# Group-major inputs, 112-row transfers and one decay load for two scans in a fused RWKV and MoE kernel

## The chip, the cores and the metric

The kernel runs on 1 core of one Trainium2 chip. The metric is the device time of one execution in microseconds (us), lower is better; the figure quoted is the median of several executions. TensorE (PE, with its weight loads shown apart as PEld), VectorE (DVE), ScalarE (ACT), GpSimd (POOL) and SyncE (SP, which here only issues DMA transfers) run side by side, each through its own list of instructions in order, and wait for one another by semaphores.

## The reference

A recurrence over 768 steps for 4 batches x 8 heads with a 40x40 state, and behind it two feed-forward blocks on 3072 tokens.

```python
for t in range(S):
    y[:, :, t] = np.einsum('bhd,bhde->bhe', rt, state)
    Sa = np.einsum('bhde,bhe->bhd', state, at)
    state_decay = state * wt[:, :, None, :] - np.einsum('bhd,bhe->bhde', Sa, bt)
    state = state_decay + np.einsum('bhd,bhe->bhde', vt, kt)
...
h = x @ w_in                                   # 3072x320 by 320x2048
x = (h * (1.0 / (1.0 + np.exp(-1.702 * h)))) @ w_out
...
h = (x @ w1) * (x @ w2) @ w3                   # 320x1024 twice, 1024x1024
out = h @ w_out2                               # 1024x320
```

## The kernel before

**The recurrence.** Time is cut into 12 chunks of 64 steps; a chunk of one batch is a group, so there are 48 groups (`NG`), numbered so that four groups in a row are the four batches of one chunk. A group's tiles hold two halves of 40 rows each, in partitions 0 to 39 and 64 to 103 (104 rows, with 24 unused ones between), and 4 head pairs x 64 steps = 256 columns per operand.

**L_part(n)** prepares the decays of group n. One transfer brings four operands of 256 columns: the decays shifted one way, the decays shifted the other way, a and b (`LA`, 104 rows of 4096 bytes, of which the DRAM array has all 48 groups side by side in each row). On DVE a scan (L453) multiplies the decays from the back, a product of 4 columns (L456) forms each head's whole decay, a reciprocal of 4 columns (L457) starts the second scan (L458), which multiplies reciprocally from the front. Then a is multiplied on POOL (L460) and b on POOL or DVE (L462, L464), the result goes to DRAM scratch (`psc`), and PE multiplies a by b into a triangular block (L476), which DVE or ACT copies out (L482, L479).

**T_part(blk)** inverts the triangular blocks of 8 groups on DVE: a transpose (L498), 30 pairs of products and sums (L514, L518), a transpose (L524), and then PE and ACT steps (L543 to L559). **J_part, V_part, S_pair** read the scratch back (`pq`, `xl`), load `jk`, `jr`, `kb`, `xy`, and run the recurrence itself, two groups at a time, on PE, DVE, ACT and POOL; S_pair's state and output are added on DVE (L732, L734) and the output is stored to DRAM (`ysc`).

**moe1(k)** is the first feed-forward block for chunk k: its input is loaded from `ysc` and split on ACT and DVE into a high and a low part (L903, L905, L915, L916); then for 16 slices f there are 8 matmuls (L958), a gelu on ACT (L962), a cast on ACT (L964), a remainder on POOL (L965), and 6 matmuls for the second layer (L942). Its result is transposed on DVE (L974). Its weights arrive as 64-bit numbers and are converted by DVE (L795, L797, L799), ACT (L793, L801, L808) and POOL (L810). **moe2(blk)** is the second block, six times 512 tokens; its matmuls (L1140, L1126) stand at the end of PE's list, behind all of the recurrence and moe1.

**What sets the order.** No engine's order is written by hand. `Plan.run` takes all operations with a cost, an engine, what each reads and writes, and a due time (`at`, made of constants such as `D1`, `TG`, `G1`, `JO`), and plays them through its own cost rules; the order in which it starts them is the order in which they stand on each engine. A transfer's cost comes from `us()`, which before is its bytes at one rate for all. So a changed cost or due time moves instructions everywhere.

All transfers but four stand on SP's one list, in the planner's order, and SP waits there for what a transfer needs.

Of the kernel before, what the change touches and what calls it, by code (L numbers as in the profile page):

```python
# [18 lines left out]
C = 64  # L19
# [28 lines left out]
G1 = 0.54  # L48
# [9 lines left out]
B1 = 0.45  # L58
# [47 lines left out]
def PO(n):  # L106
    return 0.18 + 2.15e-3 * n
# [6 lines left out]
class Plan:  # L114
# [173 lines left out]
def rwkv_moe_kernel(ctx: ExitStack, tc: tile.TileContext, LA, JK, JR, KBT, VT,  # L288
# [9 lines left out]
    psc = dp.tile([NG, 104, SC], F32, name="psc")  # L298
# [144 lines left out]
    def L_part(n):  # L443
        at = at_L(n)
        if n < NLE:
            t, nm = le[n], f"le{n}"
# [4 lines left out]
        kw, ka, kb_, kiv = nm + "w", nm + "a", nm + "b", nm + "i"
        dma(at - 1.5 * T, t[:, OQ:SC + 256], LA[:, n], w=[kw, ka, kb_, kiv])
        op("DVE", SCAN(256, 1), at, lambda: v.tensor_tensor_scan(fl(iv)[:, ::-1], fl(iv)[:, ::-1], fl(sd1)[:, ::-1], 0.0,  # L453
                                                         op0=ALU.mult, op1=ALU.max),
           r=["scan1"], w=[kiv])
# [9 lines left out]
        dma(at + (PD if n < 8 else 1.0), psc[n], t[:, 0:SC], r=[kw, kiv, ka], w=[("ps", n)])  # L465
# [117 lines left out]
    def V_part(n):  # L583
        at = sl(n) - VO * T
        i, x3, i4 = n % 2, n % 3, n % 4
        dma(at - T, fl(jr[x3]), JR[:, n], w=[f"jr{x3}"])
# [34 lines left out]
        iv = heads(pq[x3], OQ)  # L621
# [136 lines left out]
    le = [pt([104, SC + 256], f"le{i}", F32, epool) for i in range(NLE)]  # L758
# [701 lines left out]
```

## Time and profile before

| | us |
|---|---|
| median of 3 runs (1123.81 to 1129.26) | 1128.95 |
| the profiled execution, its own time | 1128.93 |
| its span, from the first to the last instruction | 1127.2 |
| PE busy in the span | 968.7 (86%) |
| ACT busy | 716.1 (64%) |
| DVE busy | 692.1 (61%) |
| POOL busy | 452.8 (40%) |

The page cuts the span into 40 slices of 28.2 us and gives for each the busy share of every engine in tenths. Shares over the whole span mix three kinds of stretches, so they are read slice by slice, and then by stretches whose ends are marked by the first instruction of a stage. The profiled execution's own time is its span and 1.7 us around it, and equals the median within 0.1 us.

### The profile page before, as it was taken

What the parts mean: (1) busy time and instruction counts of PE and PEld (TensorE: products, weight loads), DVE (VectorE), ACT (ScalarE), POOL (GpSimd) and SP (SyncE); (2) the same over time, 40 slices, a digit from 0 to 9 for tenths busy, and PEclk for the clock granted to TensorE, in tenths of its full rate; (3) what the DMA queues carried; (4) which work ended last, traced back from release to release, by engine and by line L of the source; (5) the groups of instructions that cost most, each with busy time, mean ns of one, the idle gap of its engine ahead of it and who ended that gap; (6) DMA issues with size and microseconds to landing.
All of it is one profiled execution on the core that took longest, in us unless ns stands there. A gap on an engine that the chain in (4) does not pass through costs nothing.

```text
span 1127.2 us, 31560 instructions
## 1 busy us (share of the span) xinstructions
PE 968.7 (86%) x12090; PEld 854.6 (76%) x12090; DVE 692.1 (61%) x1540; ACT 716.1 (64%) x2084; POOL 452.8 (40%) x704
## 2 busy tenths in 40 slices
PE   2137579888989999999899999978997999999996
PEld 2125368677878888888898888878895888888885
DVE  7898898669956994697468432359852433333222
ACT  4367588967887767677667876678878523223221
POOL 5455656455526655664475444544540000000000
PEclk9998569988989998999899999997998999999998
DMA  8737754578657636654444333145539222021011
GB/s 205 245 114 200 198 159 134 141 199 212 184 147 206 157 90 166 178 149 117 131 117 109 95 92 87 41 120 181 158 82 322 37 40 52 5 48 33 1 25 27
DMA packets 188560, 140.99 MB, mean 125 GB/s; under 512 B 124016, under 2 KB 159216, under 8 KB 188400
## 3 DMA queue, kind: packets, MB, share of 16 engines
q1 hardware_dynamic: 188080, 138.56, 46.2%
q8 instruction: 97, 1.59, 0.6%
q14 instruction: 63, 0.52, 0.2%
q10 hardware_dynamic: 320, 0.33, 0.1%
HBM read 109.00 MB, written 29.83 MB: 123 GB/s over the span
## 4 chain that ended last, share of the span: by engine, by line
PE 55%; DVE 19%; ACT 13%; issue 5%; DMA 5%; SPq 1%; POOL 1%; ACTq 0%; DVEq 0%; POOLq 0%
PE bank L1140 15%; PE bank L958 10%; PE bank L942 9%; PE bank L1126 7%; DVE bank L514 3%; DVE lp L518 2%; PE bank L696 2%; PE bank L728 2%; DVE st L799 2%; PE bank L476 1%; PE bank L708 1%; DVE xy L719 1%; DVE bank L797 1%; PE bank L1078 1%; DVE bank L795 1%
## 5 line engine op out<-in xcount | busy, mean ns | idle before, releaser
L965 POOL TENSOR_TENSOR gl<-xsg,gh 128x256 fp32r<-128x256 f32 x192 | 148.7, 778 | 151.4 <-ACT gh L964 114.8
L958 PE MATMUL bank<-xt,wih 128*128 128x256 f32 x768 | 164.4, 298 | 5.3 <-ACT xsg L962 4.9
L958 PEld LDWEIGHTS bank<-xt,wih 128*128 128x128 f32 x768 | 127.0, 195 | 14.3 <-ACT xsg L962 8.4
L942 PE MATMUL bank<-woh,gh 128*128 128x320 f32 x384 | 126.8, 330 | 3.8 <-DVE xo L974 2.6
L942 PE MATMUL bank<-woh,gl 128*128 128x320 f32 x384 | 125.2, 327 | 3.8 <-POOL gl L965 3.8
L942 PE MATMUL bank<-wol,gh 128*128 128x320 f32 x384 | 126.0, 328 | 0.6 <-POOL wol L810 0.6
L1146 DVE TENSOR_TENSOR sa<-bank,sa 128x512 f32<-128x512 f32 x48 | 33.2, 691 | 142.2 <-PE bank L1140 124.1
L958 PE MATMUL bank<-xt,wil 128*128 128x256 f32 x384 | 112.1, 292 | 0.0
L962 ACT ACTIVATE xsg<-bank 128x256 f32<-128x256 f32 x192 | 72.6, 382 | 60.1 <-PE bank L958 42.1
L514 DVE TENSOR_TENSOR bank<-lp 128x30 f32<-128x30 f32 (+9 forms) x180 | 82.9, 461 | 4.6
L958 PE MATMUL bank<-xt,wir 128*128 128x256 f32 x384 | 85.3, 293 | 0.3 <-issue 0.3
L964 ACT CAST gh<-xsg 128x256 fp32r<-128x256 f32 x192 | 77.3, 405 | 9.6 <-PE bank L942 6.2
L942 PEld LDWEIGHTS bank<-woh,gh 128*128 128x128 f32 x384 | 75.4, 196 | 7.8 <-DVE xo L974 3.2
L942 PEld LDWEIGHTS bank<-woh,gl 128*128 128x128 f32 x384 | 75.4, 197 | 7.0 <-POOL gl L965 4.6
L1145 ACT COPY sa<-bank 128x512 f32<-128x512 f32 x48 | 28.0, 584 | 82.2 <-PE bank L1140 82.1
L1148 ACT CAST gh<-sa 128x512 fp32r<-128x512 f32 x48 | 29.7, 619 | 77.1 <-DVE sa L1146 77.1
L942 PEld LDWEIGHTS bank<-wol,gh 128*128 128x128 f32 x384 | 75.4, 196 | 3.3 <-POOL wol L810 0.9
L958 PEld LDWEIGHTS bank<-xt,wil 128*128 128x128 f32 x384 | 75.0, 195 | 2.1 <-issue 0.7
L631 ACT COPY ivt<-bank 64x208 f32<-64x208 f32 x192 | 62.5, 325 | 15.9 <-PE bank L626 9.9
L636 POOL TENSOR_TENSOR kb<-kb,ivt 128x160 f32<-128x160 f32 x96 | 53.8, 578 | 37.9 <-ACT ivt L631 31.6
L719 DVE TENSOR_TENSOR xy<-bank,mtx 64x416 f32<-64x416 f32 x96 | 52.8, 585 | 23.4 <-PE bank L709 22.5
L958 PEld LDWEIGHTS bank<-xt,wir 128*128 128x128 f32 x384 | 62.1, 193 | 2.4 <-issue 1.2
(205 smaller groups left out, 3165.0 us busy)
## 6 DMA issues: line engine op xcount, KB each, us to landing
lw<-in_LA_dram SPq DMA_DIRECT2D x39, 416.0 KB
psc<-lw SPq DMA_DIRECT2D x39, 313.6 KB
pq<-psc SPq DMA_DIRECT2D x48, 209.6 KB
jk<-in_JK_dram SPq DMA_DIRECT2D x48, 208.0 KB
raw<-in_w3t_dram SPq DMA_DIRECT2D x32, 256.0 KB
kb<-in_KBT_dram SPq DMA_DIRECT2D x48, 160.0 KB
raw<-in_w_out_dram SPq DMA_DIRECT2D x20, 256.0 KB
jr<-in_JR_dram SPq DMA_DIRECT2D x48, 104.0 KB
```

The lines of the kernel that those rows point to most:

```text
L514: v.tensor_tensor(t, _bc(LP[:, j + 1:32, j:j + 1], [128, n, j]), _bc(LP[:, j:j + 1, 0:j], [128, n, j]), op=ALU.mult)
L631: op("ACT", AC(208), at, lambda h=h, d=d: s.copy(ivt[d:d + 64, h // 64::2], B2.t[h:h + 64, 0:208].rearrange("p (a b) -> p a b", a=2)), r=[ ...
L636: op("Pool", PO(160), at, lambda eo=eo: g.tensor_tensor(kb[:, :, eo], kb[:, :, eo], ivt[:, :, 64 * eo:64 * eo + D], op=ALU.mult), r=["ivt" ...
L719: op("DVE", VE(416), at, lambda eo=eo, r=r, xy=xy, B2=B2: v.tensor_tensor(xy[r, :, eo, :], v3(B2, 416)[r], _bc(mtx[r], [64, NP, 104]), op= ...
L942: op("PEw", MM(1, 0.1465), at(), lambda w_=w_, g_=g_, z=z, t=t: mm(acc[t].t[:, 0:DM], g_()[:, 128 * t:128 * t + 128], w_(), start=(f == 0 ...
L958: op("PEw", MM(1, 0.117), at(), lambda a=a, b=b, i=i, B=B: mm(B.t[:, 0:NF], a(), b(), start=(i == 0), stop=(i == 7)), r=ks + [f"wi{f // 2} ...
L962: op("ACT", AC(256) + 0.015, at(), lambda B=B, si=si: s.activation(sg[:, si], B.t[:, 0:NF], AF.Gelu_apprx_sigmoid), r=[B], w=[f"sg{si}"])
L964: op("ACT", AC(256) + 0.04, at(), lambda GH=GH, si=si: s.copy(GH(), sg[:, si]), r=[f"sg{si}"], w=[kg[0]])
L965: op("Pool", PO(256), at(), lambda GH=GH, GL=GL, si=si: g.tensor_tensor(GL(), sg[:, si], GH().bitcast(F32), op=ALU.subtract), r=[f"sg{si}" ...
L1126: op("PEw", MM(1, 0.1465), at(), lambda a=a, b=b, t=t, ts=ts, z=z: mm(acc[t].t[:, 0:DM], dyn[a][gi][:, ts], dyn[b][:, f], start=(f == 0 an ...
L1140: op("PEw", MM(1, 0.2325), at(), lambda a=a, k=k, b=b, i=i, B=B, fs=fs: mm(B.t, dyn[a][:, fs] if k is None else dyn[a][:, k, fs], X(b), st ...
L1146: op("DVE", VE(512), t, lambda gi=gi, B=Bs[1]: v.tensor_tensor(dyn["sa"][gi], B.t, dyn["sa"][gi], op=ALU.mult), r=[Bs[1]], w=[f"sa{gi}"])
```

## The change

Three things are edited, and the planner's constants with them.

1. **Layout.** `LA`, `JK` and `JR` lie group by group in DRAM, with 112 rows per group in place of 104 (8 padding rows). `psc` and the tiles that take these transfers have 112 rows too; compute on `pq` and `jk` keeps to 104 of them.
2. **One load of the decays.** `LA` has the decays once (`w2`), each head's first decay apart (`w0`, 4 columns) and four padding columns: 776 columns, 3104 bytes a row, for 1024 and 4096. The first scan reads `w2` and writes elsewhere; the second runs over the same `w2` in place, one column further, and starts from a reciprocal of the first scan's own head (no product ahead of it). The 4-column product moves from DVE to POOL (L461 of the new kernel), and a second 4-column reciprocal on DVE (L466) turns it into the second scan's first column.
3. **Cost of a transfer.** `us()` books rows, pieces per row and bytes per piece, divided by the largest number up to 16 that divides the rows.

```diff
-OA = OP + NP * C
+OA = OP + NP * C + 8
+RL = 112
-URGENT = 33
+URGENT = 38
-D1 = 7.0
+D1 = 8.45
-TG = 13.65
+TG = 14.85
...
-    lw = [pt([104, SC + 256], f"lw{i}") for i in range(NLW)]
+    lw = [pt([RL, SC + 256], f"lw{i}") for i in range(NLW)]
...
-        return max(0.15, n / 380.0)
+        rows, row = ap.shape[0], 4
+        for x in ap.shape[1:]:
+            row *= x
+        run = run or row
+        return max(0.1, 1e-3 * rows * (row // run) * (8 + 0.037 * run) / max(k for k in range(1, 17) if rows % k == 0))
...
-        dma(at - 1.5 * T, t[:, OQ:SC + 256], LA[:, n], w=[kw, ka, kb_, kiv])
-        op("DVE", SCAN(256, 1), at, lambda: v.tensor_tensor_scan(fl(iv)[:, ::-1], fl(iv)[:, ::-1], fl(sd1)[:, ::-1], 0.0,
-        op("DVE", VE(4, 1), at, lambda: v.tensor_tensor(heads(t, 0, 1), iv[:, :, 0:1], pl[:, :, 1:2], op=ALU.mult), r=[kw], w=[kiv])
-        op("DVE", VE(4), at, lambda: v.reciprocal(sdl[:, :, 0:1], heads(t, 0, 1)), r=[kiv], w=["sdl0"])
-        op("DVE", SCAN(256, 1), at, lambda: v.tensor_tensor_scan(fl(pl), fl(pl), fl(sdl), 0.0, op0=ALU.mult, op1=ALU.max),
+        dma(at - 1.5 * T, t[:, OP:SC + 256], LA[n], w=[kw, ka, kb_, kiv])
+        op("DVE", SCAN(256, 1), at, lambda: v.tensor_tensor_scan(fl(iv)[:, ::-1], wd[:, ::-1], fl(sd1)[:, ::-1], 0.0,
+        op("DVE", VE(4) + 0.02, at, lambda: v.reciprocal(sdl[:, :, 0:1], iv[:, :, 0:1]), r=[kiv], w=["sdl0"])
+        op("Pool", 0.2, at, lambda: g.tensor_tensor(heads(t, 0, 1), iv[:, :, 0:1], w0, op=ALU.mult), r=[kw, kiv], w=[nm + "p"])
+        op("DVE", SCAN(256, 1), at, lambda: v.tensor_tensor_scan(
+            t[:, OP + 1:OP + 1 + NP * C], t[:, OP + 1:OP + 1 + NP * C], fl(sdl), 0.0, op0=ALU.mult, op1=ALU.max),
+        op("DVE", VE(4) + 0.02, at, lambda: v.reciprocal(pl[:, :, 0:1], heads(t, 0, 1)), r=[nm + "p"], w=[kw])
...
-        dma(at - 1.5 * T, jk[i], JK[:, n], w=[kk, f"jv{i}"])
+        dma(at - 1.5 * T, jk[i], JK[n], w=[kk, f"jv{i}"])
```

Nine further constants of due times and costs (`G1`, `B1`, `T2`, `ST2`, `LAND`, `SPREAD` among them) change by small amounts. The number of instructions per engine is the same on PE, ACT, DVE and SP; POOL has 48 more. The new kernel's lines stand 3 to 9 further down (L457, L460, L463 are the old L453, L457, L458; L969, L971 the old L962, L964).

The order on DVE at the start of the program, where the first decays are prepared (`le` and `lw` are the tiles of successive groups, `scan` and `sdl` the scans' constants); before:

```order
L458 SCALAR_TENSOR_TENSOR le_146<-le_146,sdl_78 104x256
L453 SCALAR_TENSOR_TENSOR le_147<-le_147,scan_77 104x256
L456 TENSOR_TENSOR le_147<-le_147 104x4
L453 SCALAR_TENSOR_TENSOR le_148<-le_148,scan_77 104x256
L457 RECIPROCAL sdl_78<-le_147 104x4
L462 TENSOR_TENSOR le_147<-le_147 104x256
L458 SCALAR_TENSOR_TENSOR le_147<-le_147,sdl_78 104x256
L456 TENSOR_TENSOR le_148<-le_148 104x4
L453 SCALAR_TENSOR_TENSOR le_149<-le_149,scan_77 104x256
```

And now:

```order
L466 RECIPROCAL le_147<-le_147 112x4
L460 RECIPROCAL sdl_78<-le_148 112x4
L457 SCALAR_TENSOR_TENSOR le_149<-le_149,scan_77 112x256
L457 SCALAR_TENSOR_TENSOR le_150<-le_150,scan_77 112x256
L457 SCALAR_TENSOR_TENSOR le_151<-le_151,scan_77 112x256
L469 TENSOR_TENSOR le_150<-le_150 112x256
L457 SCALAR_TENSOR_TENSOR le_152<-le_152,scan_77 112x256
L457 SCALAR_TENSOR_TENSOR lw_79<-lw_79,scan_77 112x256
L469 TENSOR_TENSOR lw_79<-lw_79 112x256
L463 SCALAR_TENSOR_TENSOR le_148<-le_148,sdl_78 112x256
L466 RECIPROCAL le_148<-le_148 112x4
```

The first scans of the fourth to the eighth group now stand ahead of the second scan of the third.

On POOL in the same stretch; before:

```order
L464 TENSOR_TENSOR le_146<-le_146 104x256
L460 TENSOR_TENSOR le_146<-le_146 104x256
L460 TENSOR_TENSOR le_147<-le_147 104x256
L460 TENSOR_TENSOR le_148<-le_148 104x256
L464 TENSOR_TENSOR le_148<-le_148 104x256
L460 TENSOR_TENSOR le_149<-le_149 104x256
```

And now:

```order
L461 TENSOR_TENSOR le_146<-le_146 112x4
L471 TENSOR_TENSOR le_146<-le_146 112x256
L461 TENSOR_TENSOR le_147<-le_147 112x4
L467 TENSOR_TENSOR le_146<-le_146 112x256
L467 TENSOR_TENSOR le_147<-le_147 112x256
L461 TENSOR_TENSOR le_148<-le_148 112x4
L471 TENSOR_TENSOR le_148<-le_148 112x256
L467 TENSOR_TENSOR le_148<-le_148 112x256
```

One product of 4 columns per group has come in, among the 256-column products.

On ACT in the first moe1, from the fourth gelu on (`xsg<-bank` is the gelu, `gh<-xsg` the cast behind it; `xy`, `ivt`, `sd` belong to the recurrence, `sq`, `wih`, `woh` to the weights); before:

```order
L615 COPY xy_93<-bank_120 64x4x64
L666 COPY xy_93<-sh_106 40x4x40
L615 COPY xy_93<-bank_120 64x4x64
L631 COPY ivt<-bank_121 64x2x104
L801 ACTIVATE sq_141,GD<-sq_141,negc 128x256
L663 COPY sd_110<-bank_120 40x2x40
L962 ACTIVATE xsg<-bank_124 128x256
L663 COPY sd_110<-bank_120 40x2x40
L808 CAST wih<-st_139 128x256
L663 COPY sd_110<-bank_120 40x2x40
L964 CAST gh_162<-xsg 128x256
L663 COPY sd_110<-bank_120 40x2x40
```

And now:

```order
L969 ACTIVATE xsg<-bank_124 128x256
L800 ACTIVATE sq_142<-raw_137 128x256
L971 CAST gh_162<-xsg 128x256
L808 ACTIVATE sq_142,GD<-sq_142,negc 128x256
L815 CAST wih<-st_139 128x256
L969 ACTIVATE xsg<-bank_123 128x256
L971 CAST gh_161<-xsg 128x256
L969 ACTIVATE xsg<-bank_124 128x256
L971 CAST gh_161<-xsg 128x256
L672 COPY xy_93<-sh_106 40x4x40
L638 COPY ivt<-bank_120 64x2x104
```

Three slices of moe1(0) now run with none of the recurrence's copies between them. On PE the same holds: ahead of the last second-layer matmul of moe1(0) stand 1540 instructions before and 1332 now, ahead of that of moe1(1) 1970 and 1874, and from moe1(3) to the end of moe1 the two lists are within a few slices of each other.

## Rows read from the trace of the kernel before

**Rows 1.** The page's 40 slices of the span, busy tenths: PE, DVE, DMA.

```profile
PE   2137579888989999999899999978997999999996
...
DVE  7898898669956994697468432359852433333222
...
DMA  8737754578657636654444333145539222021011
```

**Rows 2.** Windows by stage: length, busy (instructions) per engine, clock, DMA share, GB/s.

```profile
core 0: us, PE busy (x) PEld busy (x) DVE busy (x) ACT busy (x) POOL busy (x), PEclk, DMA share, GB/s
0.00:155.40 155.40, 64.60 (x1348) 51.19 (x1348) 132.16 (x307) 92.33 (x271) 80.52 (x133) 0.84 0.67 188
155.40:247.30 91.90, 80.82 (x1409) 70.49 (x1408) 68.39 (x164) 76.13 (x237) 52.01 (x79) 0.91 0.58 160
247.30:302.10 54.80, 48.36 (x640) 42.82 (x639) 52.07 (x122) 40.64 (x128) 31.91 (x54) 0.94 0.73 190
302.10:743.50 441.40, 420.61 (x6758) 374.97 (x6757) 270.59 (x615) 323.68 (x1000) 241.17 (x379) 0.98 0.48 126
743.50:806.70 63.20, 50.87 (x314) 47.31 (x313) 56.55 (x139) 55.69 (x195) 29.40 (x39) 0.86 0.57 171
...
845.00:1127.20 282.20, 265.13 (x1349) 229.60 (x1347) 88.39 (x141) 99.48 (x170) 0.00 (x0) 0.98 0.24 59
```

**Rows 3.** Lines L958 and L905: duration ns min/median/max, first and last start.

```profile
L958 PE MATMUL bank<-xt,wih x768: 275/281/583, 155.4 to 842.0; 128*128 128x256 f32 x192
...
L905 DVE TENSOR_TENSOR xt<-xsg,xt x24: 379/426/958, 144.8 to 755.6; 128x256 fp32r<-128x256 f32 x24
```

**Rows 4.** Windows of DVE alone up to 144.8 us.

```profile
0.00:144.80 144.80, 122.18 (x284) 0.87 0.67 187
```

**Rows 5.** Timeline of DVE, 0 to 32 us: start, duration, instruction, [idle before <-releaser].

```profile
5.34 0.69 DVE L453 TENSOR_TENSOR_SCAN le<-le,scan 104x256 f32<-104x256 f32 x1 [2.29 <-DMA le<-in_LA_dram]
...
9.34 0.69 DVE L453 TENSOR_TENSOR_SCAN le<-le,scan 104x256 f32<-104x256 f32 x1 [0.81 <-DMA le<-in_LA_dram]
...
11.36 0.99 DVE L453 TENSOR_TENSOR_SCAN le<-le,scan 104x256 f32<-104x256 f32 x1 [0.30 <-DMA le<-in_LA_dram]
...
25.34 0.69 DVE L453 TENSOR_TENSOR_SCAN lw<-lw,scan 104x256 f32<-104x256 f32 x1 [0.99 <-DMA lw<-in_LA_dram]
...
29.18 0.69 DVE L453 TENSOR_TENSOR_SCAN lw<-lw,scan 104x256 f32<-104x256 f32 x1 [1.81 <-DMA lw<-in_LA_dram]
...
31.32 0.69 DVE L453 TENSOR_TENSOR_SCAN xsg<-xsg,scan 104x256 f32<-104x256 f32 x1 [1.06 <-DMA xsg<-in_LA_dram]
```

**Rows 6.** Windows as in rows 2, at the first loads and at weight loads.

```profile
3.00:13.00 10.00, 2.15 (x64) 1.67 (x64) 6.43 (x15) 7.14 (x20) 2.48 (x3) 1.00 0.85 216
...
26.00:33.00 7.00, 4.24 (x124) 3.45 (x124) 3.65 (x12) 2.82 (x9) 1.41 (x2) 1.00 0.94 258
```

**Rows 7.** Windows to 144.8 us, first of L456 alone, then of L457 alone.

```profile
0.00:144.80 144.80, 6.24 (x19) 0.87 0.67 187
...
0.00:144.80 144.80, 3.08 (x19) 0.87 0.67 187
```

**Rows 8.** Lines L456 and L457: duration ns min/median/max, first and last start.

```profile
L456 DVE TENSOR_TENSOR lw<-lw x39: 139/166/1271, 21.7 to 567.8; 104x4 f32<-104x4 f32 x39
...
L457 DVE RECIPROCAL sdl<-lw x39: 148/179/184, 22.4 to 568.5; 104x4 f32<-104x4 f32 x39
```

**Rows 9.** Groups of POOL by form: shapes, count, busy us, mean ns, idle before.

```profile
L965 POOL TENSOR_TENSOR gl<-xsg,gh 128x256 fp32r<-128x256 f32 x192 | 148.7, 778 | 151.4 <-ACT gh L964 114.8 <-issue 9.1 <-PE bank L942 7.6
...
L507 POOL MEMSET lp<- 128x32 f32 x6 | 1.0, 160 | 0.0
```

**Rows 10.** Who waited for whom: us in total, times, longest.

```profile
POOL gl L965 <- ACT gh L964: 114.8, 77, 7.0
...
DVE sh L651 <- DMA pq<-psc: 18.4, 10, 4.7
```

More of the change, by code (lines that the diff above doesn't have):

```diff
@@ L47 @@
 ST1 = 1.02
-G1 = 0.54
+G1 = 0.46
 G2 = 0.88
@@ L57 @@
 B0 = 0.42
-B1 = 0.45
+B1 = 0.41
 C0 = 41.83
@@ L66 @@
 VO = 0.84
-T2 = 3.6
-ST2 = 4.78
+T2 = 4.67
+ST2 = 5.83
 ND = 146
-TG = 13.65
+TG = 14.85
 PD = 6.02
@@ L297, in rwkv_moe_kernel @@
     x2sc = dp.tile([NCH, 2, 128, DM], F32, name="x2sc")
-    psc = dp.tile([NG, 104, SC], F32, name="psc")
+    psc = dp.tile([NG, RL, SC], F32, name="psc")
     w12sc = dp.tile([8, 3, 128, 256], F32, name="w12sc")
@@ L322, in rwkv_moe_kernel @@
     mtx = pt([128, 1, 104], "mtx")
-    sd1 = pt([104, NP, C], "scan1")
-    sdl = pt([104, NP, C], "sdl0")
-    lw = [pt([104, SC + 256], f"lw{i}") for i in range(NLW)]
-    jk = [pt([104, 512], f"jk{i}") for i in range(2)]
-    pq = [pt([104, OA], f"pq{i}") for i in range(3)]
-    jr = [pt([104, NP, C], f"jr{i}") for i in range(3)]
+    sd1 = pt([RL, NP, C], "scan1")
+    sdl = pt([RL, NP, C], "sdl0")
+    lw = [pt([RL, SC + 256], f"lw{i}") for i in range(NLW)]
+    jk = [pt([RL, 512], f"jk{i}") for i in range(2)]
+    pq = [pt([RL, OA], f"pq{i}") for i in range(3)]
+    jr = [pt([RL, NP, C], f"jr{i}") for i in range(3)]
     XL = [pt([128, NP, 2, C], f"xl{i}") for i in range(2)]
@@ L464, in L_part @@
             op("Pool", PO(256), at, lambda: g.tensor_tensor(b, b, iv, op=ALU.mult), r=[kiv], w=[kb_])
-        dma(at + (PD if n < 8 else 1.0), psc[n], t[:, 0:SC], r=[kw, kiv, ka], w=[("ps", n)])
+        dma(at + (PD if n < 8 else 1.0), psc[n], t[:, 0:SC], r=[kw, kiv, ka, nm + "p"], w=[("ps", n)])
         B = Bank("A")
@@ L620, in V_part @@
         B2 = Bank("A")
-        iv = heads(pq[x3], OQ)
+        iv = heads(pq[x3][0:104], OQ)
         def trf():
@@ L757, in rwkv_moe_kernel @@
     epool = estack.enter_context(tc.tile_pool(name="epool", bufs=1))
-    le = [pt([104, SC + 256], f"le{i}", F32, epool) for i in range(NLE)]
+    le = [pt([RL, SC + 256], f"le{i}", F32, epool) for i in range(NLE)]
     def swap0():
@@ L1409, in rows @@
         x = np.concatenate([f(x) for x in xs], axis=3)
-        o = np.zeros((104,) + x.shape[2:], np.float32)
-        o[0:D], o[64:104] = x[0], x[1]
+        o = np.zeros((NG, RL, x.shape[3]), np.float32)
+        o[:, 0:D], o[:, 64:104] = x.transpose(0, 2, 1, 3)
         return o
-    LA = rows(w2, w1, H["a"], H["b"])
+    LA = rows(z, w2, w0, z, H["a"], H["b"])
     JK, JR = np.concatenate([rows(H["k"]), rows(H["v"][::-1])], axis=2), rows(H["r"][::-1])
-    LA[D:64, :, 0:2 * NP * C] = 1.0
-    LA[D:64, :, NP * C + 1:2 * NP * C:C] = 2.0 ** -40
+    for r in (slice(D, 64), slice(104, RL)):
+        LA[:, r, 0:OA - OP] = 1.0
+        LA[:, r, NP * C + 2:NP * C + 6] = 2.0 ** -40
     def tm(x):
```

35 lines of the change are left out of this document (17 added, 18 removed).

## The prediction

> **What bounds the kernel now.** I read the 40 slices first, to see which engine is full where: DVE is at 0.7 to 0.9 from the start while PE is at 0.1 to 0.7, and from about the seventh slice PE is at 0.8 to 0.9 almost to the end [rows 1]. So I cut the span at the first and last matmuls of moe1 and took PE's idle time of each stretch, length less busy [rows 2, 3]. Up to the first matmul of moe1(0) at 155.4 us PE is idle for 155.4 - 64.6 = 90.8 us; up to the end of moe1(0) for 11.1; up to the end of moe1(1) for 6.4; in the 441 us behind that for only 20.8; in the fold of the second block's weights (743.5 to 806.7) for 12.3; and in moe2, from 845 to the end, for 17.1. Two thirds of all PE idle time lies ahead of 155 us. Behind 302 us PE is 95% busy, its work is the same in both kernels, and moe2's list is untouched, so the end moves by what PE's idle time before about 302 us loses or gains, unless a later stretch turns worse.
>
> What holds PE up until 155 us is DVE. Up to the first subtraction of moe1(0)'s input (L905) at 144.8 us [rows 3], DVE is busy for 122.18 of 144.8 us [rows 4]; the gap is 22.6. I then went through DVE's list at the start for what those gaps are [rows 5]. The first scan begins at 5.34 us. Five gaps behind it end with a load of decays: 0.81, 0.30, 0.99, 1.81 and 1.06, in all 4.97 us. Scans three and four start 2.02 us apart (9.34 and 11.36), both released by their load: that is the time of one load of 104 x 4096 = 425,984 bytes, 211 GB/s, and the window around it says 216 GB/s at a DMA share of 0.85, while a window with 128-row weight loads reaches 258 GB/s at 0.94 [rows 6].
>
> **The change, part by part.**
>
> Loads of the decays. A load is now 112 x 3104 = 347,648 bytes. At the old rate it takes 1.65 us, at the 258 GB/s of the 128-row window 1.35 us [rows 6]. I take 1.35, since 112 rows are nearer to 128-row transfers than to the old strided ones, and keep 1.65. One group costs DVE two scans (0.69 each [rows 5]; I take the second as wide as the first) and two reciprocals, 2 x 0.69 + 2 x 0.15 = 1.7 us, so a load every 1.35 us is no longer what a scan waits for, with one exception made by the new order: the eighth group's first scan now stands ahead of the third group's second scan. The first load lands 2.02 - 1.35 = 0.67 us sooner, at 4.67; the eighth at 4.67 + 7 x 1.35 = 14.1. DVE gets to the eighth scan after seven first scans, two second ones, five reciprocals and two 256-column products, for which I put about 1.0 us with no row (the scans set the sum): 9 x 0.69 + 5 x 0.15 + 1.0 = 8.0 us, at 12.7. It waits 1.4 us there, with everything behind it on DVE. So of the gaps 0.67 + 4.97 - 1.4 = 4.2 us go. Ends: 1.65 us a load makes the first gain 0.37 and that wait 16.5 - 13.0 = 3.5, 1.8 us in all; no wait at all makes it 5.6.
>
> The 4-column work. Ahead of L905's first instruction DVE has 285 instructions before and 284 now, the same but for three kinds: 19 products L456 are gone, 19 reciprocals have come, one remainder of a weight stands further back. The 19 products took 6.24 us and 19 reciprocals 3.08 [rows 7], a gain of 3.2. The remainder is only later; it has no row, I put 0.7 us, the length of a scan of as many columns. I count 3.2 + 0.7 = 3.9.
>
> POOL's 19 products of 4 columns, and a new wait. Each second reciprocal (L466) waits for POOL's product, and behind it on DVE stand the next group's scan, the weight conversions and the evictions that PE waits for. No row shows such a product. The nearest are POOL's smallest work, a fill of 32 columns, 160 ns, and a whole 256-column product standing in front of it, 778 ns [rows 9]. Where the planner leaves other DVE work between, the wait costs nothing. Ends: 0 and 19 x 0.78 = 14.8 us; I take one product's own length, 19 x 0.16 = 3.0 us lost, as it is the row nearest in size.
>
> How long DVE's two kinds of small work take shows who else is at work: the 4-column product needs 139 to 1271 ns, the reciprocal of the same size never over 184 [rows 8]. The Trainium skill, SBUF — State Buffer, "Who interferes with whom", says why: a VectorE instruction with two SBUF inputs and a GpSimd one that reads SBUF exclude each other for the whole instruction, one with a single input is free of that. It speaks for the new reciprocals and against the new POOL products, each of which may hold up a scan for its own length: by the rule 19 x 0.16 = 3.0 us more are lost and the time is 1124.5; by the rows alone the sum below stands.
>
> So moe1(0) begins 4.2 + 3.9 - 3.0 = 5.1 us sooner.
>
> New turns in 155 to 302 us. PE's list has moe1(0) as one run now, with 208 fewer instructions ahead of its end (1332 for 1540), and the recurrence pairs that stood between are behind it. PE is idle here for 11.1 + 6.4 = 17.5 us [rows 2]. All of it could not go; the pairs that come later could also make DVE and PE wait for each other. I take 2.4 us gained, a seventh, and hold -8 to +8 as ends.
>
> Transfers later on. DVE waited 18.4 us in 10 times for `pq` [rows 10]; `pq`, `psc`, `jk` and `jr` have 8% more rows over more engines. These waits lie mostly where PE is 95% busy, so I count nothing, up to 2 us gained.
>
> The rest (constants in due times behind 302 us, the fold, moe2) I count at nothing: PE's idle time there is 20.8 in 441 us, and the two lists keep step. If a stretch with little slack is put out of step, that is the second rival.
>
> Sum: 5.1 + 2.4 = 7.5 us off the profiled execution's own 1128.9, which is also the median: **1121.4 us**, 0.7% faster.
>
> **The rivals.**
>
> No change (1127 us). The gain at the start is real but moe1(0) running ahead only moves the idle time: the pairs behind it come due together, PE's 17.5 us of idle time between 155 and 302 us grow by about 5.5, and the end is 2 us sooner at most. For it: DVE is 95% busy from 247 to 302 us (52.07 of 54.8) [rows 2], so late pairs have no room there. Against it: POOL and ACT have room, and moe1(1) also ends with 96 fewer instructions ahead.
>
> Slower (1139 us). DVE is held by POOL. POOL works in order and waits often: 77 times, 114.8 us in all, for the cast in moe1 (L964) before it can form a remainder [rows 10]. A 4-column product queued behind such a wait holds DVE's second reciprocal, and with it the evictions. Of the 48 products about 27 fall before 302 us, where DVE decides. At 0.78 us each they cost 21 us, not 3.0 + a little: 1121.4 + 18 = 1139. It is slower by over 0.5% (13.1 us from my forecast) once a product costs DVE over 0.16 + 13.1 / 27 = 0.65 us on average. Against it: DVE waited for POOL's work on the decays hardly at all until now, and the planner knows of this wait.
>
> The loads are not faster (1130 us). If 211 GB/s is no matter of rows or layout but of how much is in flight, and the smaller load takes 2.02 us too, the eighth scan waits until 5.3 + 7 x 2.02 = 19.5, over 6 us, and the gain of 4.2 turns into a loss of about 4. Against it speaks 258 GB/s a few microseconds later [rows 6]. The Trainium skill, DMA: Bandwidth & Descriptors, "Why a DMA increments its semaphore by 16 and not by 1", has a transfer run on the largest number of engines up to 16 that divides its rows: 13 of 16 for 104 rows, 16 for 112. The share of 0.85 beside 13/16 = 0.81 fits that.
>
> **How the numbers follow.** Forecast 0.54 (of which 0.02 ends within 0.5%), no change 0.22, slower 0.17, loads not faster 0.07. A measurement of this kernel tells about 0.5% (5.6 us) from no change, so faster means under 1123.3 and slower over 1134.6: faster 0.52, same 0.31, slower 0.17. The range: with the kind ends (5.6 for the loads, no POOL loss, 8 in the turns) the time would be 1128.9 - 17.5 = 1111; I put the low end there. At the other side are the two rivals at 1127 and 1130 and part of the slower one; 1136 leaves out about 0.12.
>
> **What would show it.** In the new profile: DVE's gaps that end with a load of decays gone but for one of 1 to 2 us at the eighth first scan; L905's first start near 139.7 and L958's near 150; PE's idle time up to the end of moe1(1) near 101 us for 108.3; DMA share above 0.9 in the first 10 us; waits of DVE for POOL's 4-column product in the table of waits, some 3 us up to the first moe1. It would be wrong if those waits exceed 10 us, if L958 starts no sooner than 153 us, or if PE's idle time behind 302 us (50 us in all) changes by over 5 us.

## The result, and the profile after

The changed kernel takes 1115.53 us (median of 8 runs, 1113.03 to 1120.3), the kernel before 1126.15 us in the same set (8 runs): a ratio of 0.9906, 95% interval 0.9879 to 0.9934, which is 10.6 us or 0.9%. A second set (new_again below) gave 0.9919 [0.9891, 0.9947]. The forecast was 1121.4 us, 0.7% faster, with a range of 1111 to 1136.

The profiled executions stand further apart: spans of 1127.2 and 1111.8 us, 15.4 us. Over all sets before ran from 1118 to 1134 us and the new kernel from 1108 to 1120, so one pair of traces shows the places better than the sizes. Each kernel has a second trace: new_again is the new kernel once more, and lay104 has the rows and the order of the kernel before.

The slices that answer to [rows 1] (PE, DVE, DMA). In the first two slices DMA is at 9 and 6 where before it was at 8 and 7, DVE at 8 and 9 for 7 and 8, and PE at 3 and 3 for 2 and 1:

```profile
PE   3326489898989999998999999988899999999997
...
DVE  8987998688967876796486233258853333323222
...
DMA  9637654686677457645442333145538412021011
```

For the stages I take marks that both kernels have exactly: the first cast of moe1(0) on ACT (L964, now L971), and the transposes of the results of moe1(1), moe1(9) and moe1(11) on DVE (L974, now L981). Windows of the kernel before, columns as in [rows 2]:

```profile
0.00:158.20 158.20, 67.40 (x1361) 53.97 (x1362) 134.76 (x314) 93.00 (x273) 81.24 (x134) 0.84 0.67 187
158.20:304.10 145.90, 126.81 (x2036) 110.70 (x2036) 119.79 (x283) 116.70 (x366) 84.69 (x133) 0.93 0.64 172
304.10:743.10 439.00, 419.77 (x6752) 374.39 (x6752) 268.26 (x611) 323.03 (x997) 239.27 (x376) 0.98 0.48 125
743.10:844.90 101.80, 89.47 (x599) 85.85 (x598) 80.78 (x195) 83.86 (x280) 47.57 (x62) 0.92 0.49 144
844.90:1127.20 282.30, 265.23 (x1349) 229.70 (x1348) 88.49 (x142) 99.48 (x170) 0.00 (x0) 0.98 0.24 59
```

The same five of the new kernel:

```profile
0.00:150.80 150.80, 66.73 (x1356) 53.81 (x1356) 130.51 (x311) 93.66 (x273) 83.29 (x151) 0.92 0.67 189
150.80:284.10 133.30, 121.03 (x1850) 105.31 (x1848) 111.27 (x266) 108.97 (x345) 81.47 (x132) 0.92 0.66 179
284.10:731.50 447.40, 428.71 (x6943) 380.75 (x6944) 276.38 (x631) 331.00 (x1019) 251.41 (x408) 0.97 0.49 127
731.50:839.50 108.00, 91.68 (x599) 85.77 (x598) 78.45 (x197) 85.66 (x283) 46.94 (x62) 0.94 0.49 141
839.50:1111.80 272.30, 263.12 (x1349) 228.35 (x1347) 87.90 (x140) 97.61 (x168) 0.00 (x0) 0.99 0.24 59
```

The length of a window less PE's busy time is PE's idle time. Before it is 90.8, 19.1, 19.2, 12.3 and 17.1 us; now 84.1, 12.3, 18.7, 16.3 and 9.2. So PE lost 6.7 us of idle time ahead of moe1, 6.8 in the first two moe1, 0.5 in the long middle and 3.9 from there to the end, 18 us in all; its busy time is 2.6 us more. The second trace of the new kernel has 84.9, 12.9, 17.9, 15.7 and 9.1 us, and lay104's trace 90.8, 18.3, 16.2, 12.9 and 16.6. So the middle is uncertain by some 3 us, and the other stretches repeat within 1 us. The granted clock of the first window, 0.92 for 0.84, is not what brings moe1 forward: new_again has 0.86 up to 149 us, and its first cast comes at 149.8.

At the start of DVE's list the scans, answering to [rows 5]:

```profile
4.50 0.69 DVE L457 TENSOR_TENSOR_SCAN le<-le,scan 112x256 f32<-112x256 f32 x1 [1.44 <-DMA le<-in_LA_dram]
...
5.44 1.26 DVE L463 TENSOR_TENSOR_SCAN le<-le,sdl 112x256 f32<-112x256 f32 x1
...
13.30 0.66 DVE L457 TENSOR_TENSOR_SCAN lw<-lw,scan 112x256 f32<-112x256 f32 x1
...
17.14 0.73 DVE L457 TENSOR_TENSOR_SCAN lw<-lw,scan 112x256 f32<-112x256 f32 x1 [0.48 <-DMA lw<-in_LA_dram]
```

The first scan starts 0.84 us sooner. Of the waits for loads behind the first scan, six before (the five of [rows 5] and one of 0.17 us), only one of 0.48 us is left up to 32 us, and the eighth first scan (13.30) doesn't wait. But the second scan (L463) takes 1.26 us where I had put 0.69.

First starts of moe1's matmuls and of the subtraction ahead of them, answering to [rows 3]:

```profile
L965 PE MATMUL bank<-xt,wih x768: 275/281/583, 145.6 to 836.5; 128*128 128x256 f32 x192
```

```profile
L912 DVE TENSOR_TENSOR xt<-xsg,xt x24: 395/426/1000, 138.1 to 747.1; 128x256 fp32r<-128x256 f32 x24
```

The subtraction starts at 138.1 us for 144.8, and the first matmul at 145.6 for 155.4.

### The profile page after: what moved, and what is told of

The parts are those of the page before. It is cut to its first block, busy times and chain, and to the rows that moved or that the text cites. A ratio compares the mean times of both kernels' runs of the same rounds, so it can differ in the third digit from the quotient of the medians.

```text
span 1111.8 us, 31653 instructions
## 1 busy us (share of the span) xinstructions
PE 971.3 (87%) x12090; PEld 854.0 (77%) x12090; DVE 684.5 (62%) x1540; ACT 716.9 (64%) x2084; POOL 463.1 (42%) x752
## 4 chain that ended last, share of the span: by engine, by line
PE 54%; ACT 17%; DVE 16%; issue 5%; DMA 4%; POOL 2%; SPq 0%; ACTq 0%; DVEq 0%; POOLq 0%
PE bank L1147 14%; PE bank L965 10%; PE bank L949 9%; PE bank L1133 7%; DVE bank L521 3%; PE bank L703 2%; PE bank L735 2%; DVE lp L525 2%; PE bank L1085 2%; ACT sd L670 2%; PE bank L483 2%; ACT ivt L638 1%; PE bank L715 1%; DVE xy L726 1%; DVE st L806 1%
## 5 line engine op out<-in xcount | busy, mean ns | idle before, releaser
L972 POOL TENSOR_TENSOR gl<-xsg,gh 128x256 fp32r<-128x256 f32 x192 | 149.3, 781 | 152.7 <-ACT gh L971 134.7
L965 PE MATMUL bank<-xt,wih 128*128 128x256 f32 x768 | 167.6, 298 | 5.7 <-ACT xsg L969 5.7
L969 ACT ACTIVATE xsg<-bank 128x256 f32<-128x256 f32 x192 | 73.1, 383 | 67.2 <-PE bank L965 51.9
L971 ACT CAST gh<-xsg 128x256 fp32r<-128x256 f32 x192 | 77.4, 404 | 7.6 <-PE bank L949 4.5
```

The source lines that it names most:

```text
L965: op("PEw", MM(1, 0.117), at(), lambda a=a, b=b, i=i, B=B: mm(B.t[:, 0:NF], a(), b(), start=(i == 0), stop=(i == 7)), r=ks + [f"wi{f // 2} ...
L969: op("ACT", AC(256) + 0.015, at(), lambda B=B, si=si: s.activation(sg[:, si], B.t[:, 0:NF], AF.Gelu_apprx_sigmoid), r=[B], w=[f"sg{si}"])
L971: op("ACT", AC(256) + 0.04, at(), lambda GH=GH, si=si: s.copy(GH(), sg[:, si]), r=[f"sg{si}"], w=[kg[0]])
L972: op("Pool", PO(256), at(), lambda GH=GH, GL=GL, si=si: g.tensor_tensor(GL(), sg[:, si], GH().bitcast(F32), op=ALU.subtract), r=[f"sg{si}" ...
```

## The experiments

My theory was that 112 rows make the loads faster, that DVE is rid of 19 products, and that the new turns of the first moe1 add a little; by turns I mean the order in which the planner puts the operations on each engine. The rivals: the loads are not faster or hidden anyway, POOL's products hold DVE up, or the turns carry nearly all. Ratios are to the kernel before, run on the same chip in the same set.

### Rows and layout, with every engine's order held

Three kernels are the one before with other inputs; the planner was given the old cost of each transfer, so every engine's list stands as it was. The rows are those of all transfers that the change gives 112 rows (`LA`, `JK`, `JR`, and the scratch `psc` that is written and read back), not of the decays' loads alone.

lay112, group by group and 112 rows (cut to `LA` and its tiles; `JK`, `JR`, `psc` and theirs change likewise):

```diff
+RL = 112
...
-    lw = [pt([104, SC + 256], f"lw{i}") for i in range(NLW)]
+    lw = [pt([RL, SC + 256], f"lw{i}") for i in range(NLW)]
...
-        dma(at - 1.5 * T, t[:, OQ:SC + 256], LA[:, n], w=[kw, ka, kb_, kiv])
+        dma(at - 1.5 * T, t[:, OQ:SC + 256], LA[n], w=[kw, ka, kb_, kiv])
```

> The kernel before with one edit: inputs group by group and 112 rows a transfer, its own columns (4096 bytes a row), every engine's order as before. A load is now 458,752 bytes. Theory (rows and layout make the rate): at the 279 GB/s of the new kernel's window from 3 to 13 us a load takes 1.64 us for 2.02, the gaps of DVE that end with a load up to 32 us fall from 4.97 us to 2 to 3.5, L905 starts 2 to 3.5 us earlier, the median is 1 to 4 us under the kernel before. Rival (the rate is set by what is in flight, the new kernel's loads are faster only because they are smaller): 211 GB/s, 2.17 us a load, the gaps grow by about 1 us, median 0 to 2 us over.

lay104, the layout alone, with `RL = 104`:

> As lay112 but with 104 rows: layout alone, every engine's order as before. If the number of rows makes the rate: window 3 to 13 us at a DMA share of 0.85 and about 216 GB/s as before, the gaps on loads within 0.7 us of 4.97, median within 3 us of before. If the layout makes it: over 250 GB/s and the same gain as lay112.

str112, the rows alone, with the arrays' layout of before:

> As lay112 but with the groups side by side in each DRAM row as before: 112 rows alone, every engine's order as before. If the number of rows makes the rate: DMA share near 1.0 and 250 to 279 GB/s in the window 3 to 13 us, gain as lay112 (1 to 4 us). If the layout makes it: as before, 216 GB/s.

And the new kernel with both undone, new_str104, its own order held:

```diff
-RL = 112
+RL = 104
...
-        dma(at - 1.5 * T, t[:, OP:SC + 256], LA[n], w=[kw, ka, kb_, kiv])
+        dma(at - 1.5 * T, t[:, OP:SC + 256], LA[:, n], w=[kw, ka, kb_, kiv])
```

> The new kernel with one part undone: inputs side by side and 104 rows a transfer again, every engine's order as in the new kernel. A load is 322,816 bytes, 1.50 us at 216 GB/s for 1.25 at 279. My theory: DVE's waits for loads up to the first L912 grow by 2 to 4 us from 4.9, and the median is 2 to 4 us above the new kernel (1117.5 to 1119.5). Rival (the new turns make nearly all of the gain and the loads are hidden in this order): within 1 us of the new kernel.

The window from 3 to 13 us of lay104, str112, lay112, new_str104 and the new kernel, in this order (columns as in [rows 6], where before has 0.85 and 216 GB/s):

```profile
3.00:13.00 10.00, 2.16 (x64) 1.67 (x64) 6.55 (x16) 7.26 (x21) 2.47 (x3) 1.00 0.85 220
```

```profile
3.00:13.00 10.00, 2.15 (x64) 1.67 (x64) 7.74 (x19) 7.53 (x21) 4.10 (x5) 1.00 1.03 299
```

```profile
3.00:13.00 10.00, 2.16 (x64) 1.68 (x64) 7.69 (x19) 7.53 (x21) 4.05 (x5) 1.00 1.04 280
```

```profile
3.00:13.00 10.00, 2.16 (x64) 1.68 (x64) 7.64 (x16) 7.52 (x21) 4.31 (x7) 1.00 0.86 216
```

```profile
3.00:13.00 10.00, 2.15 (x64) 1.67 (x64) 8.49 (x17) 7.53 (x21) 4.74 (x7) 1.00 1.03 279
```

The last two columns settle it: every kernel with 104 rows has a DMA share of 0.85 or 0.86 and 216 to 220 GB/s, every one with 112 rows 1.03 or 1.04 and 279 to 299. Neither the layout nor the bytes of a row (4096, or 3104 in the last two) carries a kernel from one group to the other. The times follow: lay104 1.0005 [0.9979, 1.0031], str112 0.9949 [0.9927, 0.9972], lay112 0.9939 [0.9912, 0.9967]. In str112 and lay112 the subtraction of moe1(0)'s input first starts at 139.7 and 140.9 us for 144.8. DVE's waits for loads up to 144 us, before and in lay112 (line L453 is L454 there):

```profile
DVE le L453 <- DMA le<-in_LA_dram: 3.6, 4, 2.3
DVE lw L453 <- DMA lw<-in_LA_dram: 2.8, 2, 1.8
...
DVE xsg L453 <- DMA xsg<-in_LA_dram: 1.1, 1, 1.1
```

```profile
DVE le L454 <- DMA le<-in_LA_dram: 2.0, 1, 2.0
...
DVE xsg L454 <- DMA xsg<-in_LA_dram: 0.6, 1, 0.6
```

So in the old order rows alone are worth 0.5 to 0.6%, some 6 us, over the 1 to 4 I had written.

What they are worth in the new order is less certain. new_str104, which undoes rows and layout, has 0.9938 [0.992, 0.9956] against 0.9906 and 0.9919: a difference of 0.2 to 0.3%, 2 to 4 us, which is what I expected but is about as large as its own uncertainty. Its trace points the same way: DVE waits 7.9 us for loads up to 144 us for the new kernel's 4.9, and the first cast of moe1(0) comes at 154.1 us for 150.8.

### The turns

> The new kernel once more, beside the other runs of this set on one chip: its ratio to the kernel before within 0.9875 to 0.9935, and PE's idle time up to the end of moe1(1) 93 to 100 us against 109.9 in the first profile of before.

It gave 0.9919, and 97.8 us of idle time.

Two kernels have one half of the change each. oldplan has the new data and instructions, newplan the new constants and transfer cost:

```diff
# oldplan, from the new kernel
-D1 = 8.45
+D1 = 7.0
-TG = 14.85
+TG = 13.65
...
-        return max(0.1, 1e-3 * rows * (row // run) * (8 + 0.037 * run) / max(k for k in range(1, 17) if rows % k == 0))
+        return max(0.15, n / 380.0)
# newplan, from the kernel before: the same lines the other way round
```

> The new kernel's data and instructions (112 rows, one load, products of 4 columns on POOL), but turns by the constants and the transfer cost of before. My theory: the 112 rows (5 to 7 us by the two kernels that had 112 rows in the old order) and the fewer products on DVE (3 us) come in any order: ratio to before 0.990 to 0.994. Rival (the new turns are what makes the gain): 0.996 to 1.000.

> The kernel before with only the new constants and the new transfer cost: its data, its 104 rows and its 4-column products on DVE as they were, the turns new. My theory: turns alone are worth 0 to 3 us, ratio 0.997 to 1.001, loads of 104 rows still 2.0 us apart. Rival (turns carry the 6.8 us that PE's idle time lost from 151 to 284 us): 0.993 to 0.996.

Both theories missed. newplan is slower, 1.0106 [1.0073, 1.0139], and oldplan too, 1.0057 [1.0036, 1.0079], though each has half of a change that gains 0.9%. The data under the old constants lose 0.6%; the new constants and the new cost of a transfer take 1.4% off that. (There are nine such constants, `LAND` and `SPREAD` among them: beyond the three that the diff of the change shows, six and not nine.) So the constants are not a refinement on top of the edits: the edits change costs, the planner deals out all turns anew, and without the constants the new turns are bad.

What tells oldplan from the new kernel shows at one place. The first matmul of moe2 (L1140, there L1145) waits for DVE's low part of its input (`xtb`); before, and then oldplan, waits of PE behind 740 and 800 us:

```profile
PE bank L1140 <- DVE xtb L915: 6.6, 1, 6.6
```

```profile
PE bank L1145 <- DVE xtb L920: 12.4, 1, 12.4
```

In the new kernel this wait is not there. It goes with the turns and not with the rows: lay104, lay112 and str112, which keep the old order, have it with 6.5 to 6.9 us, and new_str104 and dve4_fixed (below), which keep the new one, don't have it. PE's idle time from moe1(9)'s end to the end is 25.5 us, before 29.4, in oldplan 31.3. The rest of what oldplan loses against the new kernel lies in small pieces: the first gelu comes at 156.4 us for 149.4, since DVE has 328 instructions ahead of the first cast for 311 (first of the rows below, to be held against the first of the new kernel's five), and PE's busy time is 4 us longer.

```profile
0.00:157.50 157.50, 69.12 (x1415) 55.88 (x1416) 139.09 (x328) 97.25 (x285) 89.42 (x160) 0.84 0.66 192
```

Why oldplan is slower than before these pieces don't tell. Its trace has less idle time of PE than before (152.7 us for 158.5, and for 154.8 in lay104), and more busy time (975 us for 969 and 971). The granted clock over its 12 runs is 0.944 on average, and 0.9545 over the 23 of before; no run separates the clock from the turns, so this stays open.

newplan's trace doesn't name a wait. Its idle time is that of before (158.4 us for 158.5), but PE is busy for 982 us for 969, with the clock lower in the first two moe1 (0.88, in the second of before's five rows 0.93):

```profile
162.30:313.40 151.10, 134.30 (x2084) 117.13 (x2085) 123.65 (x287) 120.96 (x372) 86.81 (x135) 0.88 0.64 170
```

That is one execution, the slowest of newplan's six, and the mean clock over its six runs (0.956) is not below that of before (0.9545), so the clock is not shown to be the cause. Why these turns are slow on the old data stays open. It is also one set of constants on the old data: whether another would have gained there, with none of the edits, no run has tried.

Which part of the constants' half matters, new_oldus tells apart: the new kernel with the old transfer cost, and the old `LAND` and `SPREAD` beside it.

> The new kernel with the old cost of a transfer (bytes at one rate) and the old two constants beside it (LAND 3.5, SPREAD 1.5); the other constants are the new ones. If the constants set the turns that gained: 0.990 to 0.995. If the cost of a transfer does, or both only fit together: 1.000 to 1.010.

0.9921 [0.9895, 0.9948], the same as the new kernel. Booking transfers by rows and pieces is worth nothing that can be measured here, although it moves thousands of instructions; the other seven constants make the difference of 1.4% to oldplan. But new_oldus gets there in another way. Its first gelu comes as late as oldplan's:

```profile
L967 ACT ACTIVATE xsg<-bank x192: 361/384/402, 156.3 to 831.8; 128x256 f32<-128x256 f32 x192
```

PE's idle time is 146.6 us in it for 140.6 in the new kernel, and the granted clock over its six runs 0.969 for 0.956. So a late first gelu doesn't by itself make a kernel late, and part of what the booking is worth may be hidden behind the clock.

### The 4-column product

dve4 puts the product back on DVE and plans again; dve4_fixed issues it on DVE at the place where POOL has it, and moves nothing else:

```diff
# dve4
-        op("Pool", 0.2, at, lambda: g.tensor_tensor(heads(t, 0, 1), iv[:, :, 0:1], w0, op=ALU.mult), r=[kw, kiv], w=[nm + "p"])
+        op("DVE", VE(4, 1), at, lambda: v.tensor_tensor(heads(t, 0, 1), iv[:, :, 0:1], w0, op=ALU.mult), r=[kw, kiv], w=[nm + "p"])
# dve4_fixed
-        op("Pool", 0.2, at, lambda: g.tensor_tensor(heads(t, 0, 1), iv[:, :, 0:1], w0, op=ALU.mult), r=[kw, kiv], w=[nm + "p"])
+        op("Pool", 0.2, at, lambda: v.tensor_tensor(heads(t, 0, 1), iv[:, :, 0:1], w0, op=ALU.mult), r=[kw, kiv], w=[nm + "p"])
```

> The new kernel with the product of 4 columns on DVE in place of POOL (planned again with that). My theory: 19 products up to the first moe1 at 0.33 us (6.24 us in 19 before) put 4 to 6 us back on DVE: first gelu 4 to 6 us later than the new kernel's 149.4, ratio to before 0.993 to 0.996. Rival (POOL's small products are what makes the second scans long, 0.99 us a scan for 0.80 before): the second scans go back to 0.8 us, 3.7 us in 19, and the ratio is 0.988 to 0.991.

> The new kernel with the 48 products of 4 columns issued on DVE at the place in the program where POOL has them; every other instruction stands where it stood. It tells the price of the swap alone from that of the other turns that came when the planner was let loose on it (ratio 1.000 there). My theory: 19 products up to the first moe1 at 0.2 to 0.33 us put 4 to 6 us on DVE, the first gelu comes 3 to 5 us later than 149, ratio to before 0.994 to 0.997. Rival (the swap is worth nothing, the other turns made the difference): 0.989 to 0.993.

dve4 gives 1.0002 [0.9985, 1.002], dve4_fixed 0.9936 [0.9912, 0.9961]. Against the new kernel's 0.9906 and 0.9919 the swap alone comes to 0.2 to 0.3%, 2 to 3 us, no more than the uncertainty of that difference; its trace agrees with the sign: the 19 products take DVE 6.22 us again, and the first gelu comes at 151.6. The other 0.65% of dve4 is turns dealt out anew: PE is idle for 150.6 us in its trace, for 144.9 in dve4_fixed. The rival of dve4, that POOL's small products make the second scans long, falls: in dve4 POOL has none, and 19 second scans still take 18.50 us.

### What makes the second scans long

In the new kernel 19 second scans (L463) ahead of the first moe1 take 18.82 us, before 15.11 (L458). Two kernels keep every engine's order and put something else in the place of POOL's 256-column products, L467 and L471. They leave the products out, and each has one run, so only the places in their traces are used:

```diff
# pool_one (and the same for a)
-lambda: g.tensor_tensor(b, b, iv, op=ALU.mult)
+lambda: g.tensor_scalar(b, b, 0.5, None, op0=ALU.mult)
# pool_fill (and the same for a)
-lambda: g.tensor_tensor(b, b, iv, op=ALU.mult)
+lambda: g.memset(b, 0.0)
```

> The new kernel, but POOL's 256-column products on the decays (a by the reciprocal scan, b by the scan) read one operand instead of two (multiplied by the constant 0.5, so the products are left out). Every engine's order is the same. Theory (any POOL instruction that reads SBUF holds a scan with two SBUF operands up): the 19 second scans ahead of the first moe1 still take 0.9 us or more on average (0.99 to 1.02 in the new kernel). Rival (only a POOL instruction with two operands does): 0.69 to 0.75.

> The new kernel, but POOL's 256-column products on the decays are fills with zero, which read nothing (the products are left out). Every engine's order is the same. Theory (POOL's reading of SBUF is what makes the second scans long): the 19 second scans ahead of the first moe1 take 0.69 to 0.75 us on average, 4 to 5 us less in all, the reciprocals as before, and the first gelu comes 3 to 5 us before 149.4. Rival (they are long from something else, the odd start column of the in-place scan among it): still 0.95 or more.

DVE's second scans alone, window up to 149 us (length, busy, clock, DMA share, GB/s), of before, the new kernel, pool_one and pool_fill in this order:

```profile
0.00:149.00 149.00, 15.11 (x19) 0.86 0.66 185
```

```profile
0.00:149.00 149.00, 18.82 (x19) 0.92 0.67 192
```

```profile
0.00:149.00 149.00, 14.91 (x19) 0.87 0.67 192
```

```profile
0.00:149.00 149.00, 14.13 (x19) 0.87 0.67 192
```

With fills the scans are back at 14.13 / 19 = 0.74 us, so the in-place scan from an odd column isn't slow; POOL's reading is what holds it. With one operand it is 0.78 on average, which neither theory had: a scan beside POOL is held, but less. The first scans (L457) gain nothing from the fills, 13.52 us in 19 for 13.57. One pair each, POOL and DVE in order of time, of the new kernel, of pool_one and of pool_fill (the DVE row stands further down):

```profile
5.42 0.72 POOL L471 TENSOR_TENSOR le<-le 112x256 f32<-112x256 f32 x1
...
5.44 1.26 DVE L463 TENSOR_TENSOR_SCAN le<-le,sdl 112x256 f32<-112x256 f32 x1
```

```profile
5.48 0.85 POOL L471 TENSOR_SCALAR le<-le 112x256 f32<-112x256 f32 x1
...
5.49 0.94 DVE L463 TENSOR_TENSOR_SCAN le<-le,sdl 112x256 f32<-112x256 f32 x1
```

```profile
5.43 0.31 POOL L471 MEMSET le<- 112x256 f32 x1
```

Beside the two-operand product the scan takes 0.57 us longer than 0.69, beside the one-operand one 0.25, beside the fill, which runs at the same time but is shorter, none. The Trainium skill, SBUF — State Buffer, "Who interferes with whom", has a VectorE instruction with two SBUF inputs contend with a GpSimd one that reads SBUF and not with one that only writes it; pool_fill agrees (0.74 us). That the number of GpSimd's operands counts, as pool_one shows, it doesn't say. The prediction took from it that the two exclude each other for the whole instruction; here they don't, since beside a POOL instruction of 0.85 us the scan is 0.25 us longer.

What this costs is the other half of the answer. pool_fill takes 4.7 us off the second scans, and yet its first gelu comes at 149.9 us, no sooner than the 149.4 of the new kernel. DVE's list at the start of pool_fill:

```profile
5.46 0.69 DVE L463 TENSOR_TENSOR_SCAN le<-le,sdl 112x256 f32<-112x256 f32 x1
...
10.84 0.69 DVE L457 TENSOR_TENSOR_SCAN le<-le,scan 112x256 f32<-112x256 f32 x1 [0.59 <-DMA le<-in_LA_dram]
...
12.10 0.69 DVE L457 TENSOR_TENSOR_SCAN le<-le,scan 112x256 f32<-112x256 f32 x1 [0.25 <-DMA le<-in_LA_dram]
...
13.42 0.69 DVE L457 TENSOR_TENSOR_SCAN lw<-lw,scan 112x256 f32<-112x256 f32 x1 [0.64 <-DMA lw<-in_LA_dram]
...
17.62 0.69 DVE L457 TENSOR_TENSOR_SCAN lw<-lw,scan 112x256 f32<-112x256 f32 x1 [1.37 <-DMA lw<-in_LA_dram]
```

It waits for the loads instead: the first scans of the sixth, seventh and eighth group start 10.84, 12.10 and 13.42, one load each 1.26 to 1.32 us. The eighth starts 0.1 us later than in the new kernel, where the scans were slower and no load was waited for. So at the start DVE's long scans and the loads cover each other. Up to 138 us DVE waits 8.1 us for loads in pool_fill and 4.9 in the new kernel, so the loads take back 3.2 of the 4.7 us; what takes the rest isn't shown.

## Why the prediction was right, point by point

**What bounds the kernel.** It held for the new kernel: PE's idle time ahead of moe1(1)'s end fell from 109.9 to 96.4 us, and the end moved with it. I had given 101 as the sign, on a mark for which before stood at 108.3; the fall is 13.5 us (12.1 in the second trace) for the 7.3 forecast. It held for the rows too (104.0 and 106.0 us in lay112 and str112 for 109.1 in lay104, and some 6 us off the end). It isn't a rule for any order: oldplan has 104.0 us and is slower than before. Two readings were off: 90.8 of 158.5 us is 57% of all idle time and not two thirds, and behind the first scan DVE had six gaps that end with a load, the sixth of 0.17 us.

**Loads, -4.2 us.** Right in the mechanism, and shown by the three kernels in the old order. At 279 GB/s a load is 347,648 / 279,000 = 1.25 us for my 1.35. But the size was 2.6 us and not 4.2: DVE's waits for loads up to the first moe1 fell from 7.5 to 4.9 us (3.6 in the second trace). In the old order rows alone took 4.9 of the 7.5 off (2.6 are left in lay112), in the new one 3.0 of 7.9 (new_str104 against the new kernel). The new kernel's waits:

```profile
DVE lw L457 <- DMA lw<-in_LA_dram: 3.5, 2, 3.0
...
DVE le L457 <- DMA le<-in_LA_dram: 1.4, 1, 1.4
```

The wait of 1.4 us that I put at the eighth first scan didn't come, because DVE came there late with its long second scans; one of 3.0 us came instead between 100 and 120 us (the second trace has 1.8 as its longest), which I hadn't seen in the order.

**The 4-column work, -3.9 us.** Right: 19 products of 6.24 us are gone, and the reciprocals went from 3.08 to 3.01 + 3.18 = 6.19 us, a loss of 3.1 us against the 6.24, so a gain of 3.1 for the forecast 3.2 [rows 7]. The 0.7 for the remainder that stands further back is near 0.64 to 0.71 us, the mean of such a remainder (L816, L823) in the two traces.

**POOL's products, +3.0 us.** Wrong in the cause. A product takes 0.20 us alone and 5.66 / 19 = 0.30 on average, for my 0.16; but DVE waited for one only once in the whole run, 2.1 us between 300 and 400 us. What DVE lost to POOL is 3.7 us in the second scans, beside the 256-column products, which I had not costed as a term. The first scans, on the other hand, are 1.6 us shorter (13.57 us in 19 for 15.13), so both together lost 2.2 us (3.1 in the second trace); that this is near 3.0 is luck. My other sentence, by which the 4-column products hold scans up for 3.0 us more, had the kind of hold-up right and the wrong products: without them on POOL, in dve4_fixed, both kinds of scan together take 31.3 us for 32.4. That the rows gave the first scan's 0.69 for the second was my choice; before, too, some second scans took 0.9 us.

**moe1(0) 5.1 us sooner.** Its first subtraction came 6.7 us sooner. But the terms as measured, 2.6 + 3.1 - 3.7, give only 2.0 of these. The rest was in no term of mine: the first scans' 1.6 us, and above all DVE's wait for the triangular blocks from PE, up to the subtraction, before and now:

```profile
DVE ls L482 <- PE bank L476: 6.3, 4, 2.7
```

```profile
DVE ls L489 <- PE bank L483: 2.0, 2, 1.4
```

These 4.3 us come from the new turns: lay112, in the old order, still has 6.3 us, and new_str104, in the new one, 2.0. So it is partly luck that 5.1 came near 6.7.

Its first matmul came 9.8 us sooner. Part of the 3.1 us in between are turns too: before, DVE has four of the recurrence's products (L719) in front of the last parts of moe1's input, now one.

```profile
152.12 2.20 DVE L719 TENSOR_TENSOR xy<-bank,mtx 64x416 f32<-64x416 f32 x4
```

```profile
146.06 0.59 DVE L726 TENSOR_TENSOR xy<-bank,mtx 64x416 f32<-64x416 f32 x1
```

**New turns, -2.4 us.** The sign was right and the size too small: PE's idle time in the first two moe1 fell by 6.8 us (6.2 in the second trace), near the end of -8 that I kept. Rows alone, in the old order, leave it at 17.6 and 18.3 us (lay112, str112) for 19.1, so it is the order that counts there. With the 4.3 us ahead of moe1(0) this is the term that I had much too small.

**Transfers later on.** As forecast nothing: the waits of DVE for `pq` [rows 10] are 17.5 us in 12 times for 18.4 in 10. POOL's waits for the cast, the ground of the second rival, even grew, from 114.8 us to 134.7, but DVE waited for a 4-column product only that once.

**The rest at nothing.** Wrong by some 4 to 5 us. Behind moe1(1) PE's idle time is 44.2 us for 48.6 (42.7 in the second trace, 45.7 in lay104): 7.9 us less in the last window, where the wait of 6.6 us at the head of moe2 is gone, and 4.0 more in the window ahead of it, where the weights are folded. I had taken moe2 as untouched because its list is. The sign that I had set, 5 us, stands between the 4.4 of the first trace and the 5.9 of the second. I take it that the wait at moe2's head depends on how DVE's and ACT's work on moe1's last chunks stands; the runs show that it goes with the order, and not which instruction decides it.

**The sum.** The total came out near, 10.6 us for 7.5, but with the weights wrong. In the trace the loads and the 4-column work gave 5.7 us on DVE and the second scans took 3.7 back; the turns, for which I had 2.4 of 7.5 us, gave 4.3 us ahead of moe1(0), most of 6.8 in the first two moe1 and some 4 behind. By the medians, undoing the rows in the new order costs 0.2 to 0.3%, undoing the swap 0.2 to 0.3%, undoing the booking of transfers nothing, and undoing all constants and the booking 1.4%. The first two differences are each uncertain by 0.2 to 0.3%, and the parts don't add up, since an edit and its turns belong together; how the 0.9% divides is not shown.

**The rivals.** "No change" fell: moe1 ahead of the recurrence made no new idle time. "Slower" fell: 19 products, and no wait. "The loads are not faster" fell by lay104 against str112; its price was off, too: by its own numbers 4.97 us are gone and a wait of 19.5 - 13.3 = 6.2 us comes, a loss of some 1 us and not 4, so 1127 us and not 1130. The rule that I cited for it, the largest number of engines up to 16 that divides the rows (the Trainium skill, DMA: Bandwidth & Descriptors, "Why a DMA increments its semaphore by 16 and not by 1"), agrees with the measured shares: 0.85 at 104 rows and 1.03 at 112, a ratio of 1.21, for 16 / 13 = 1.23.

## What to carry to other kernels

A transfer's row count can be worth more than its layout: go by the DMA share of the first window, and test it with the order held fixed. When a planner sets the order, an edit and its due times are one change: either half alone made this kernel slower by 0.6 to 1.1%, and what an edit is worth in place (0.2 to 0.3% for the product) was swamped by the turns dealt out anew (0.65%). And ask of every engine that is late what is late right behind it: 4.7 us taken off the scans brought the first gelu no sooner, and the loads took back 3.2 of them.

## What the hardware showed beyond what I had expected

- A scan with two SBUF operands (112 x 256) takes 0.69 us alone and 1.26 beside a two-operand POOL product of the same size, 0.94 beside a one-operand one, and 0.69 beside a fill.
- POOL's product of 112 x 256 by a constant takes longer (0.85 us) than the product of two tensors (0.72).
- Groups side by side in each DRAM row, 48 x 4096 = 196,608 bytes from row to row, moved about as fast as groups laid out by themselves: 299 against 280 GB/s at 112 rows, 216 against 220 at 104.
